# A fused LayerNorm, linear-attention and gated-MLP kernel: the first LayerNorm in eight groups of two tiles, without GpSimd's -mean*rs products, and a new order of the first tasks

## The chip, the cores and the metric

The kernel runs on one core of a Trainium2 chip. The time is the device time of one execution in microseconds, the median of the timed runs. A core has five engines that run their own queues of instructions in order and wait for each other by semaphores: PE (TensorE, matrix products; its weight loads are the profile's PEld), DVE (VectorE), ACT (ScalarE), POOL (GpSimd) and SP (SyncE, which here issues nearly all DMAs). Matrix products write to PSUM, eight banks; the rest lies in SBUF.

## The reference

x has 2048 rows (tokens) of 512; all inputs are bf16. With D = 512, 32 heads of 16 and F = 1376:

```python
mod = (_silu(c) @ w_mod).reshape(c.shape[0], 6, 1, -1)
sa, ca, ga, sb, cb, gb = (mod[:, i] for i in range(6))
h = _layernorm(x) * (1 + ca) + sa
x = x + ga * _A_ref(h, A_wqkv, A_w_phi, A_wo)
h = _layernorm(x) * (1 + cb) + sb
x = x + gb * _B_ref(h, B_w_gate, B_w_up, B_w_down)
```

_layernorm is (x - mean) / sqrt(var + 1e-5) over a row. _A_ref is linear attention: q, k and v are h @ wqkv; q and k go through w_phi, a 16x16 matrix for each head, and then phi = [softmax(p), softmax(-p)]; kv = phi_k^T v, z = the sum of phi_k, the output phi_q kv / (phi_q z), times wo. _B_ref is (sigmoid(h @ w_gate) * (h @ w_up)) @ w_down.

## The kernel before

The 2048 rows are 16 tiles of 128 rows. The work is a graph of some 1200 named tasks, each with an engine and a function that issues its instructions. Which engine runs a task, and in which order, is written out by hand in the string ORDER: Graph.arrange walks through it, takes for each task the engine behind "@" (A for ACT, D for DVE, P for POOL) or else the first one that the task allows, and gives each buffer a slot, the one that has been free longest in this order. So ORDER sets the queue of each engine, and also which task must wait for a PSUM bank until an earlier user of that bank is done. A task with no "@" runs on its first alternative: phi, wo, wd, and xn1 (but for tile 0) on POOL; qphi, n, r, hm1 and foldc as their tables say.

The stages at the start, with the names used below (t is a tile, g a group of tiles of the first LayerNorm, j a quarter of the 512 columns):

- ld_x0a to ld_x3a load x in pieces of 256 KB, two tiles each (ld_x3a is 512 KB, four tiles); ld_wk0 and ld_wk1 load the key weights, ld_wm00a to ld_wm01b the first columns of w_mod (256 KB each), ld_wv0 the value weights (512 KB). wqT0 to wqT3 load the query weights and transpose them in the DMA. All are issued by SP in ORDER's order.
- warm0 and warm1_i are matrix products without use on the zeroed last block of wd_sb, to keep PE busy.
- c1, c2, c3 make silu(c) on PE, ACT and DVE. modc1.0 and modc1.1 multiply it with w_mod on PE (16 products with one column each); modc1c0 and modc1c1 copy the results to modc.
- tpw transposes the key weights on PE, wTc copies them back, fold multiplies them with the block-diagonal w_phi, foldc copies the folded weights to wqk_f, so that K gives the features' logits directly. fold0 does the same for the query weights.
- st1_t (L702, L703, DVE) makes the mean and variance of tile t. rs1_g makes 1/sqrt(var + eps) for the tiles of a group: on ACT as Ln and Exp (L709, L710), on POOL as an addition and a power (L712, L713). nmr1_g (L718, DVE) makes -mean*rs, one instruction for each tile. xn1_t normalises a tile: on ACT or POOL as x*rs + nmr (L727, L731), on DVE, tile 0 alone, as (x - mean)*rs (L729).
- tphgj (L744) transposes column block j of a group on PE, all its tiles into one bank, and hm1_gj scales it with 1 + ca and adds sa on the way to h1T (L751 on ACT, L753 on DVE). Two groups (TD) are transposed by DMA (xT1_t) and scaled in place.
- K, V and Q are the products for tile t, four matmuls of 512 columns each; Kta and Ktb are the halves. e (ACT, L776) is exp of both signs from PSUM, n (DVE, L780) the sums over a head, r the reciprocal (DVE, or Ln and Exp on ACT), phi the product; va (ACT, L836) copies V out of PSUM. kv (PE, L282) adds phi^T v into two banks over all tiles.
- kvn and kvz (DVE) copy kv out; num, rd and u make the quotient for each tile, out multiplies with wo, and the MLP follows. Its loads are ld_wg0, ld_wu0, ld_wd; wo0 to wo3 (L851) scale wo by ga, on POOL.

The groups are

```python
LG = [[0], [1], [2, 3], [4, 5], [6, 7], [8, 9], [10, 11], [12, 13], [14, 15]]
TD = [0, 0, 0, 0, 0, 0, 1, 1, 0]
```

so tiles 0 and 1 are a group each, and from the third on a group's number is half its first tile plus one.

Of the kernel before, what the change touches and what calls it, by code (L numbers as in the profile page):

```python
# [160 lines left out]
def kernel(  # L161
# [535 lines left out]
    for g, ts in enumerate(LG):  # L697
# [17 lines left out]
        if g:  # L715
            def f_nm(e, ts=ts):
                for t in ts:
                    dve.tensor_scalar(nmr[:, 0, t:t + 1], mv1[:, t, 0:1], rs1[:, t:t + 1], -1.0, op0=ALU.mult, op1=ALU.mult)  # L718
# [340 lines left out]
```

## Time and profile before

| | |
|---|---|
| median of 3 timed runs | 203.72 us (203.69 to 203.81) |
| the profiled execution, its own time | 205.47 us |
| its span, first to last instruction | 203.7 us, 4159 instructions |
| mean granted TensorE clock | 0.992 |
| DMA | 22.94 MB, mean 113 GB/s |

One execution is recorded by the hardware profiler. Times in it count from the first instruction. "Busy" is the time in which an engine had an instruction under way; instructions overlap, so the sum of their durations is more. A timeline gives for each run of like instructions the start, the time, the line of the kernel, and in brackets the idle time before and what ended it. The chain of waits follows the end of the program back: each piece is what the next one waited for, or what stood before it on its engine. The profiled execution's own time is that of the whole execution, with what lies around its span.

### The profile page before, as it was taken

Reading aid. Unit: us, or ns where it says so; the run is one execution under the profiler, and the core shown is the slowest. Engines: PE = TensorE matmul, PEld = TensorE weight load, DVE = VectorE, ACT = ScalarE, POOL = GpSimd, SP = SyncE. Lnnn points to the kernel's source line nnn. Section 1 sums busy time; section 2 is a strip of 40 time slices with the busy share of each in tenths; the row PEclk is TensorE's granted clock in tenths of the full one; section 3 lists DMA queues with packets and bytes.
Section 4 is the critical chain, followed back from the end, with each engine's and each line's share of the span. In section 5 each row is a group of like instructions: output and inputs, shape, how many; then the busy total and the mean of one; then the engine's idle time right before and its main releaser. Section 6 shows DMA issues by size and latency. Waiting matters only on the chain.

```text
span 203.7 us, 4159 instructions
## 1 busy us (share of the span) xinstructions
PE 197.0 (97%) x1471; PEld 107.0 (53%) x1471; DVE 160.6 (79%) x375; ACT 106.1 (52%) x252; POOL 102.8 (50%) x144
## 2 busy tenths in 40 slices
...
PEclk9987999999999999999999999999999999999999
...
DMA packets 49453, 22.94 MB, mean 113 GB/s; under 512 B 38065, under 2 KB 47634, under 8 KB 49426
## 3 DMA queue, kind: packets, MB, share of 16 engines
...
q8 instruction: 13, 0.21, 0.5%
q14 instruction: 14, 0.11, 0.2%
q10 hardware_dynamic: 530, 0.02, 0.1%
HBM read 11.58 MB, written 2.10 MB: 67 GB/s over the span
## 4 chain that ended last, share of the span: by engine, by line
PE 79%; DMA 8%; ACT 5%; SPq 3%; DVE 3%; issue 1%
PE y_ps L485 19%; PE u_ps L447 18%; PE g_ps L447 17%; PE k_ps L817 6%; PE a_ps L356 6%; DMA wg_sb<-in_B_w_gate_dram 5%; PE v_ps L821 4%; DMA wmod_sb<-in_w_mod_dram 3%; PE q_ps L871 3%; ACT e L776 2%; PE num L326 2%; SPq L537 1%; PE g_ps L449 1%; PE tp_h L744 1%; PE kvacc L282 1%
## 5 line engine op out<-in xcount | busy, mean ns | idle before, releaser
L457 ACT ACTIVATE tg<-g_ps 128x512 bf16<-128x512 f32 (+5 forms) x66 | 28.8, 455 | 67.0 <-PE g_ps L447 39.4
L485 PE MATMUL y_ps<-wd_sb,wmod_sb 128*128 128x512 bf16 (+4 forms) x187 | 45.7, 366 | 0.0
L468 DVE SCALAR_TENSOR_TENSOR wmod_sb<-tg,u_ps 128x512 bf16<-128x512 bf16 (+4 forms) x63 | 30.2, 491 | 18.2 <-ACT tg L457 11.6
L447 PEld LDWEIGHTS <-wg_sb 128*128 128x128 bf16 (+1 forms) x252 | 21.9, 99 | 16.1
L447 PEld LDWEIGHTS <-wu_sb 128*128 128x128 bf16 (+1 forms) x252 | 21.9, 99 | 16.0 <-issue 0.3
L784 POOL TENSOR_TENSOR qphi<-qe,qks 128x512 bf16<-128x512 bf16 x24 | 25.1, 1060 | 3.9 <-DMA pT<-qphi 1.2
L485 PEld LDWEIGHTS <-wmod_sb 128*128 128x128 bf16 (+1 forms) x187 | 17.1, 98 | 16.0 <-issue 0.6
L447 PE MATMUL u_ps<-wT_sb,wu_sb 128*128 128x512 bf16 (+2 forms) x124 | 23.8, 322 | 0.0
L447 PE MATMUL g_ps<-wT_sb,wg_sb 128*128 128x512 bf16 (+2 forms) x124 | 23.1, 322 | 0.0
L447 PE MATMUL g_ps<-wqk_sb,wg_sb 128*128 128x128 bf16 (+4 forms) x128 | 20.0, 287 | 0.0
L447 PE MATMUL u_ps<-wqk_sb,wu_sb 128*128 128x128 bf16 (+4 forms) x128 | 19.8, 287 | 0.1
L780 DVE TENSOR_REDUCE ks<-e 128x64 f32<-128x1024 bf16 (+2 forms) x22 | 19.1, 904 | 0.4 <-ACT e L776 0.4
L780 DVE TENSOR_REDUCE qks<-qe 128x64 bf16<-128x1024 bf16 x16 | 19.2, 1204 | 0.0
L492 DVE TENSOR_TENSOR ot<-y_ps,x 128x512 bf16<-128x512 f32 (+2 forms) x17 | 11.0, 653 | 10.3 <-PE y_ps L485 10.2
L376 POOL TENSOR_SCALAR ve<-mv 128x2 f32<-128x2 f32 (+1 forms) x8 | 1.8, 221 | 33.8 <-DVE mv L366 33.7
L776 ACT ACTIVATE e<-k_ps 128x512 bf16<-128x512 f32 (+2 forms) x44 | 18.0, 515 | 0.0
L817 PE MATMUL k_ps<-wqk_f,h1T 128*128 128x512 bf16 x64 | 17.9, 402 | 0.0
L776 ACT ACTIVATE qe<-q_ps 128x512 bf16<-128x512 f32 x32 | 17.4, 618 | 0.6 <-POOL phi L787 0.4
L356 PE MATMUL a_ps<-wo_sb,oT 128*128 128x512 bf16 x64 | 16.3, 379 | 0.0
L787 POOL TENSOR_TENSOR phi<-e,kr 128x1024 bf16<-128x1024 bf16 (+2 forms) x10 | 14.4, 1449 | 3.6 <-ACT kr L795 2.1
L821 PE MATMUL v_ps<-wv_sb,h1T 128*128 128x512 bf16 x64 | 16.1, 379 | 0.0
L871 PE MATMUL q_ps<-wqk_f,h1T 128*128 128x512 bf16 x64 | 15.9, 379 | 0.0
...
## 6 DMA issues: line engine op xcount, KB each, us to landing
...
wu_sb<-in_B_w_up_dram SPq DMA_DIRECT2D x1, 1376.0 KB, 11.0
...
```

The lines of the kernel that those rows point to most:

```text
L356: pe.matmul(ap_[:], lhsT=oT[:, j, :], rhs=wo_sb[:, j, :], start=(j == 0), stop=(j == KT - 1))
L447: pe.matmul(ps[:fsz, 0:n], lhsT=w[:, j, ft * P:ft * P + fsz], rhs=h[:, j, 0:n], start=(j == 0), stop=(j == KT - 1))
L457: G.add(f"tg{k}.{ft}", {"ACT": 0.13 + n * 0.00083}, lambda e, tg=tg, g_ps=g_ps, fsz=fsz, n=n: act.activation(tg[:fsz, 0:n], g_ps[:fsz, 0:n ...
L468: dve.scalar_tensor_tensor(hm_all[:fsz, hm[k].slot, ft, 0:n], tg[:fsz, 0:n], 1.0, u_ps[:fsz, 0:n], op0=ALU.add, op1=ALU.mult)
L485: mm = pe.matmul(y[:, 0:c1 - c0], lhsT=hm_all[:fsz, hm[k].slot, ft, tl * P:(tl + 1) * P], rhs=wd_sb[:fsz, ft, c0:c1], start=(ft == 0), sto ...
L776: act.activation(ee[:, a:b, s].rearrange("p g f h -> p g (f h)"), kp[:, a * 64:b * 64].rearrange("p (g n) -> p g n", n=64), ACT.Exp, scale ...
L780: dve.tensor_reduce(ks[:, a:b].rearrange("p g s h -> p (g s) h"), ee[:, a:b].rearrange("p g s f h -> p (g s) h f"), axis=AX.X, op=ALU.add)
L784: engine(e).tensor_tensor(ph[:].rearrange("p (g s f h) -> p g s f h", s=2, f=DH, h=4)[:, :, s], ee[:, :, s], ks[:, :, 1 - s].unsqueeze(2). ...
L787: engine(e).tensor_tensor(ph[:, a * P:b * P].rearrange("p (g f h) -> p g f h", f=DH, h=4), ee[:, a:b].rearrange("p g s f h -> p (g s) f h" ...
L817: pe.matmul(kp[:], lhsT=h1T[:, j, t * P:(t + 1) * P], rhs=wqk_f[:, j, D:2 * D], start=(j == 0), stop=(j == KT - 1))
L821: pe.matmul(vp[:], lhsT=h1T[:, j, t * P:(t + 1) * P], rhs=wv_sb[:, j, :], start=(j == 0), stop=(j == KT - 1))
L871: pe.matmul(qp[:], lhsT=h1T[:, j, t * P:(t + 1) * P], rhs=wqk_f[:, j, 0:D], start=(j == 0), stop=(j == KT - 1))
```

## The change

Tiles 0 and 1 become one group, so there are eight groups of two, and a group's number is half its first tile; tiles 10 to 13 still go through the DMA transposes. rs1_0 now waits for both tiles' statistics. A single product nmr1, for tile 1, is left: tile 1 is normalised by ACT, tile 0 by DVE, and all others by POOL, which now computes (x - mean)*rs from the statistics and no longer x*rs + nmr. warm1 has 13 tasks, not 12. The tasks ahead of wd0, 439 before and 424 after, stand in a new order, with some engines changed; behind them the order is the same.

```diff
-LG = [[0], [1], [2, 3], [4, 5], [6, 7], [8, 9], [10, 11], [12, 13], [14, 15]]
-TD = [0, 0, 0, 0, 0, 0, 1, 1, 0]
+LG = [[t, t + 1] for t in range(0, NT, 2)]
+TD = [0, 0, 0, 0, 0, 1, 1, 0]
...
 ORDER = """
-wdz pmem warm0 ld_x0a st1_1 rs1_1 st1_0 c1 c2 ld_x0b warm1_0 warm1_1 warm1_2 warm1_3 ld_wk0 ld_wk1 nmr1_1 xn1_1@A st1_3 warm1_4 st1_2 rs1_0 xn1_0 tph11 tpw1
-tpw0 ld_x1b ld_x1a wTc1 warm1_5 tpw2 ld_wm00b c3 tph10 tph03 tph00 st1_7 tpw3 bd rs1_2@P tph13 wTc0 nmr1_2 xn1_3 xn1_2 warm1_6 ld_wm00a st1_6 wTc2 st1_4 st1_5
-wTc3 fold11 fold10 warm1_7 foldc11 ld_x2b fold13 warm1_8 st1_11 foldc10 fold12 warm1_9 foldc13 modc1.0 warm1_10 ld_wm01b tph20 foldc12 warm1_11 rs1_4@P nmr1_4
-ld_wm01a modc1c0 hm1_11@A hm1_10@A tph02 rs1_3@P tph01 tph23 hm1_20@A hm1_01@A st1_10 tph21 hm1_21@A hm1_00 modc1.1 modc1c1@D rs1_6 nmr1_3 tph22 tph12 ld_x2a
-wqT1 hm1_22 hm1_13@A hm1_03 xn1_7 K1a K0a hm1_02@A hm1_23@A xn1_6 tph42 tph40 xn1_5 hm1_40@A st1_8 tph41 ld_x3a xn1_4 K3a hm1_42 hm1_12@A ld_wv0 nmr1_6 tph43
-K3b hm1_41@A xn1_11 tph30 xn1_10 st1_9 rs1_5@P hm1_30@A tph31 wqT3 tph32 K1b ld_wmga st1_15 st1_14 hm1_31@A fold01 foldc01 K0b tph33 wqT2 rs1_8@P K2a K2b hm1_33
-nmr1_5 V0a wqT0 V0b V3a xn1_9 e3.0 V1a xT1_11 e0.0 fold03 n3.0 V1b nmr1_8 xn1_14 va0 e2.0 n0.0 st1_13 r0.0 modca.0 modca.1 xn1_15 st1_12 xn1_8 foldc03 n2.0
-modcac e1.0 hm1_32@A V2a fold02 phi0.0 n1.0 r1.0 fold00 V2b foldc02 foldc00 r3.0 va1 xT1_10 hm1_60@P ld_wmm2 va2 r2.0@A hm1_62@P tph82 hm1_82@A tph50 phi2.0@D
-phi1.0@D hm1_50@A hm1_63@P V3b K4a K4b rs1_7@P Q0 Q2 kv0.0 Q1 qe0.0 va3 qe2.0 hm1_43@A qe1.0 modc2.0 tph52 modc2.1 tph51 nmr1_7 xn1_12 xn1_13 phi3.0@D ld_wo
-qn0.0 modc2c e4.0 kv1.0 qn2.0 hm1_52 kv2.0 Q4 K5a kv3.0 xT1_12 xT1_13 qphi0.0@P qphi0.1@P qn1.0 qe4.0 qphi2.1 tph80 K5b hm1_80@A hm1_51@A e5.0 pT0 qphi2.0 n4.0
-r4.0@A qn4.0 n5.0 phi4.0@D qphi1.1@P hm1_61@P qphi1.0@P tph53 V5 K7a V4 va5 hm1_53@A V6 pT2 hm1_70@P qphi4.1 va4 hm1_71 mask4 va6 K6a K7b K6b e6.0 K8 tph83
-hm1_83 r5.0 qphi4.0@P e8.0 pT1 pT4 ld_wd2 tph81 hm1_81 n6.0 n8.0 e7.0 n7.0 V7 kv4.0 hm1_72@P K11 K9 V9 K14 V8 r6.0@A e9.0 va7 va9 r7.0@A e11.2 e11.6 phi5.0
-phi6.0 hm1_73@P n9.0 r9.0@A kv5.0 gwa gra gwb e11.4 e14.0 K10 phi7.0@D kv6.0 K12 V10 kv7.0 e14.4 r8.0 n11.6 n11.2 r11.6 phi9.0 e10.0 e12.0 ld_wd ld_wu0 grb
-n11.4 n14.0 r11.2 n14.4 r14.0 n10.0 r14.4@A phi8.0 va8 V11 V14 n12.0 e11.0 K13 n11.0 phi11.6 r11.4 wo1 r11.0 va10 r10.0@A va11 kv8.0 kv9.0 phi11.2@D phi11.0@D
-phi10.0@D phi11.4@D V12 K15 e13.0 wmod_free ld_wg0 phi14.4 phi14.0 kv10.0 kv11.4 kv11.6 Q6 kv11.0 e13.4 r12.0@A e15.4 n13.0 n13.4 r13.0 r13.4 n15.4 e15.0 va14
-V15 V13 qe6.0 va12 kv11.2 n15.0 r15.0 r15.4@A va13 phi13.4 Q5 phi15.4 phi13.0@D va15 phi15.0@D phi12.0@D wo0 wo3 Q3 kv12.0 kv13.0 kv14.0 kv15.0 qn6.0 kvn0 kvz0
-kv13.4 kv14.4 kv15.4 kvz1 kvn1 num0a num1a num2a wo2 rd0a wo_all rd1a qe3.0 u0a num0b num4a num1b rd0b Q11 qe5.0 rd2a u0b u2a rd4a num2b qn3.0 u1a rd1b tpo0 Q8
-qphi6.0@P qphi6.1@P oT0 out0 num4b rd2b u1b wd0 qe11.0 u2b qphi3.1@P qphi3.0@P x1_0 rd4b st2_0 qe8.0 Q7 qe7.0 tpo1 oT1 Q10 Q9 out1 Q15 oT2 rs2_0 qn5.0 nmr2_0
...
+wdz pmem bd warm0 ld_x0a ld_x0b c1 st1_0 st1_1 rs1_0 warm1_0 st1_3 nmr1 xn1_1 c2 st1_2 rs1_1@P xn1_3 xn1_2 warm1_1 warm1_2 warm1_3 warm1_4 warm1_5 ld_wk0 tpw0
+wTc0 tpw1 wTc1 warm1_6 ld_x1a warm1_7 warm1_8 warm1_9 ld_wk1 tpw3 c3 warm1_10 wTc3 xn1_0 tph00 tpw2 fold11 wTc2 fold10 fold13 foldc10 foldc13 ld_x1b fold12
+tph01 warm1_11 st1_5 foldc12 st1_4 rs1_2@P xn1_4 xn1_5 st1_7 foldc11 st1_6 rs1_3 xn1_7 xn1_6 warm1_12 tph13 ld_x2b tph10 tph11 ld_wm00b ld_wm00a modc1.0 st1_11
+modc1c0@D hm1_11 tph22 hm1_10 ld_wm01b hm1_01@A tph20 tph12 hm1_20@A st1_10 rs1_5@P xn1_11 xn1_10 ld_wm01a hm1_00@A tph03 tph02 modc1.1 modc1c1@D hm1_13 K3a
+hm1_02@A hm1_03@A ld_x3a st1_15 ld_x2a st1_8 K0a st1_14 rs1_7@P hm1_12@A hm1_22@A tph23 K1a K2a K0b e0.0 ld_wv0 K3b st1_9 rs1_4@P xn1_8 K1b e1.0 e3.0 V3a V3b
+tph21 tph30 V0a st1_13 V0b va0 hm1_21 hm1_23 n0.0 K2b e2.0 tph32 hm1_32 K5a wqT2 fold02 foldc02 va3 hm1_30@A V1a V2a r0.0 V1b wqT3 wqT0 fold03 foldc03 wqT1
+fold01 foldc01 fold00 tph31 V2b n2.0 foldc00 va2 n3.0 xT1_11 st1_12 xn1_9 tph43 xn1_15 xn1_14 va1 xT1_10 r2.0@A K4a K4b tph72 hm1_72 n1.0 r1.0 phi0.0 hm1_50@P
+hm1_52@P hm1_51@P hm1_31@A rs1_6@P xn1_13 xn1_12 Q0 qe0.0 Q2 hm1_43@A qe2.0 kv0.0 phi2.0@D K5b ld_wmga Q1 phi1.0@D modca.0 modca.1 qn0.0 qe1.0 kv1.0 r3.0
+phi3.0@D modcac e5.0 V4 qn1.0 kv2.0 e4.0 ld_wmm2 modc2.0 tph33 hm1_33@A kv3.0 qphi0.1@P xT1_13 tph40 qn2.0 qphi2.0 qphi0.0@P hm1_40@A tph41 hm1_41@A gwa modc2.1
+modc2c xT1_12 va4 Q4 qe4.0 pT0 qphi2.1@P n4.0 tph42 V6 r4.0@A hm1_42 n5.0 K6a K6b qn4.0 hm1_53 phi4.0@D va6 qphi1.1@P qphi1.0@P pT2 ld_wd2 hm1_61@P qphi4.1
+tph70 K8 hm1_70@A r5.0 mask4 qphi4.0@P tph71 e6.0 n6.0 V5 va5 V9 pT1 e8.0 hm1_71 n8.0 pT4 kv4.0 K7a K7b e7.0 K9 V7 V11 e9.0 r6.0@A va9 va7 K11 e11.4 n7.0 r7.0@A
+n9.0 hm1_63@P hm1_62@P phi5.0 tph73 hm1_73 kv5.0 K10 phi6.0 V8 phi7.0@D hm1_60@P kv6.0 K14 V10 kv7.0 e11.0 r9.0@A phi9.0 e11.2 n11.4 n11.0 n11.2 r11.2 e10.0
+r8.0 r11.4@A e14.0 e11.6 n10.0 n11.6 n14.0 r14.0 va8 e14.4 K12 e12.0 phi8.0 r11.0 K15 r11.6 K13 n14.4 va11 n12.0 kv8.0 kv9.0 phi11.4@D Q6 V12 r10.0@A phi11.0@D
+phi11.2@D e13.4 r14.4@A phi10.0@D e13.0 va10 n13.0 n13.4 V14 r13.4 r13.0 ld_wo gwb gra wo1 va12 e15.4 e15.0 phi11.6 phi14.4 kv10.0 kv11.4 qe6.0 phi14.0 r12.0@A
+n15.4 r15.4@A kv11.0 kv11.2 Q5 V15 kv11.6 V13 n15.0 r15.0 phi13.0@D phi12.0@D va14 phi15.0@D phi13.4 Q3 va13 qn6.0 kv12.0 va15 kv13.0 kv14.0 kv15.0 phi15.4
+kv13.4 kv14.4 kv15.4 kvz0 kvn0 num0a kvz1 kvn1 num1a rd0a u0a qe5.0 num0b rd0b u0b num4a num2a Q8 rd4a wo2 num2b tpo0 num1b qe3.0 Q11 wo3 rd1a u1a wo0 oT0
+ld_wg0 wo_all grb ld_wd out0 num4b rd2a u2a wmod_free rd1b qn3.0 rd2b ld_wu0 qphi6.0@P u1b qphi6.1@P wd0 qe11.0 u2b qphi3.1@P qphi3.0@P x1_0 rd4b st2_0 qe8.0 Q7
...
                 pe.matmul(ps[:], lhsT=wd_sb[:, FT - 1, 0:P], rhs=wd_sb[:, FT - 1, :], start=True, stop=True)
         G.add(nm, {"PE": dur}, f, bufs=[ps], **kw)
     warm("warm0", 6, 2.4, r=["wdz"], w=["warm"])
-    for i in range(12):
+    for i in range(13):
         warm(f"warm1_{i}", 1, 0.22, r=["c1"], w=["warm"])
 
     def modc_task(nm, chs, rks, wk, f2, dur):
...
                 pool.tensor_scalar(ve1[:, sl], mv1[:, sl, 1], 1e-5, None, op0=ALU.add)
                 pool.tensor_tensor(rs1[:, sl], ve1[:, sl], mhalf[:, sl], op=ALU.pow)
         G.add(f"rs1_{g}", {"ACT": 0.43, "POOL": 1.1}, f_rs, r=[("mv1", t) for t in ts], w=[("rs1", g)])
-        if g:
-            def f_nm(e, ts=ts):
-                for t in ts:
-                    dve.tensor_scalar(nmr[:, 0, t:t + 1], mv1[:, t, 0:1], rs1[:, t:t + 1], -1.0, op0=ALU.mult, op1=ALU.mult)
-            G.add(f"nmr1_{g}", {"DVE": 0.02 + 0.1 * n}, f_nm,
+        if g == 0:
+            G.add("nmr1", {"DVE": 0.12}, lambda e: dve.tensor_scalar(nmr[:, 0, 1:2], mv1[:, 1, 0:1], rs1[:, 1:2], -1.0, op0=ALU.mult, op1=ALU.mult),
                   r=[("rs1", g)], w=[("nmr1", g)])
         for t in ts:
             xn = Buf("xn", [P, D], BF16, "xn")
...
             def f_xn(e, t=t, xn=xn):
                 if e == "ACT":
                     act.activation(xn[:], x_sb[:, t, :], ACT.Identity, scale=rs1[:, t:t + 1], bias=nmr[:, 0, t:t + 1])
-                elif e == "DVE":
-                    dve.tensor_scalar(xn[:], x_sb[:, t, :], mv1[:, t, 0:1], rs1[:, t:t + 1], op0=ALU.subtract, op1=ALU.mult)
                 else:
-                    pool.tensor_scalar(xn[:], x_sb[:, t, :], rs1[:, t:t + 1], nmr[:, 0, t:t + 1], op0=ALU.mult, op1=ALU.add)
-            G.add(f"xn1_{t}", {"POOL": 0.69, "ACT": 0.73} if t else {"DVE": 0.3}, f_xn, r=[("rs1", g)] + ([("nmr1", g)] if t else []), w=[("xn1", t)],
+                    engine(e).tensor_scalar(xn[:], x_sb[:, t, :], mv1[:, t, 0:1], rs1[:, t:t + 1], op0=ALU.subtract, op1=ALU.mult)
+            G.add(f"xn1_{t}", {"ACT": 0.73} if t == 1 else {"POOL": 0.69} if t else {"DVE": 0.3}, f_xn, r=[("rs1", g)] + ([("nmr1", g)] if t == 1 else []), w=[("xn1", t)],
                   bufs=[xn], port=("POOL", "DVE"))
         if TD[g]:
             for q, t in enumerate(ts):
```

58 lines of the change are left out of this document (29 added, 29 removed).

## The prediction

> **What bounds the kernel now.** First the page's busy shares and its row of the granted TensorE clock, in 40 slices of 5.1 us.
>
> ```profile
> span 203.7 us, 4159 instructions
> PE 197.0 (97%) x1471; PEld 107.0 (53%) x1471; DVE 160.6 (79%) x375; ACT 106.1 (52%) x252; POOL 102.8 (50%) x144
> PEclk9987999999999999999999999999999999999999
> ```
>
> PE is busy 97% of the span, and its clock dips only in slices 2 and 3. The windows, cut at that dip, show the stages (columns: length, busy of PE, PEld, DVE, ACT, POOL, clock, DMA share, GB/s).
>
> ```profile
> 10.85:14.26 3.41, 2.92 (x48) 1.85 (x47) 3.23 (x14) 3.12 (x11) 3.24 (x7) 1.00 1.26 218
> 14.26:17.68 3.42, 3.42 (x16) 1.76 (x15) 3.14 (x10) 2.54 (x7) 2.60 (x5) 0.50 1.15 345
> 17.68:24.20 6.52, 6.52 (x63) 3.92 (x61) 5.33 (x14) 6.07 (x14) 5.20 (x9) 1.00 1.25 217
> 24.20:25.10 0.90, 0.71 (x5) 0.27 (x4) 0.86 (x3) 0.90 (x3) 0.68 (x2) 1.00 1.06 403
> 25.10:58.60 33.50, 33.50 (x315) 18.37 (x315) 33.29 (x60) 32.62 (x92) 27.70 (x28) 1.00 0.73 201
> 77.00:190.00 113.00, 113.00 (x714) 59.63 (x712) 84.13 (x193) 37.58 (x77) 39.05 (x56) 1.00 0.32 62
> ```
>
> From 17.68 on PE never rests, but for the stretch at 24.2. From 25.1 to 58.6 three engines are full at once: PE 33.50 of 33.50, DVE 33.29, ACT 32.62. So time can come only from the first 25 us, and whatever PE gains there lasts only if DVE and ACT gain as much. The chain of waits says what starts the work.
>
> ```profile
> 7.07 6.14 DMA wmod_sb<-in_w_mod_dram
> 13.26 0.55 PE modc_ps L630 x16
> 13.81 0.33 PE tp_h L744 x3
> 14.14 1.46 PE k_ps L817 x4
> 15.60 0.64 PE tp_h L744 x6
> ...
> 25.08 0.27 PE tp_h L744 x2
> ...
> 25.78 0.86 PE k_ps L817 x4
> ```
>
> The eleventh load of 256 KB (ld_wm01a) lands at 7.07 + 6.14 = 13.21; modc1.1 needs it, and K1a follows at 14.14. Four K matmuls take 0.86 at 25.78: 0.215 each, or 0.43 at half clock. A transpose takes 0.64 / 6 = 0.107 at half clock, so 0.054 at full. The half-clock stretch, 3.42 us of a full PE, costs 1.7 us.
>
> **The change part by part.** Prices (groups by shape up to 58.6 us: busy, mean ns, idle before), then pitches from the timelines, where one instruction starts before the last has ended.
>
> ```profile
> L718 DVE TENSOR_SCALAR nmr<-mv,rs 128x1 f32<-128x1 f32 x15 | 2.4, 200 | 0.0
> L753 DVE TENSOR_SCALAR h1T<-tp_h,modc 128x256 bf16<-128x256 bf16 x6 | 2.3, 389 | 0.9 <-PE tp_h L744 0.9
> L753 DVE TENSOR_SCALAR h1T<-tp_h,modc 128x128 bf16<-128x128 bf16 x2 | 0.7, 334 | 0.0
> L731 POOL TENSOR_SCALAR xn<-x_sb,rs,nmr 128x512 bf16<-128x512 bf16 x14 | 11.0, 796 | 3.6 <-DVE nmr L718 1.4 <-issue 1.2 <-ACT h1T L751 0.8
> L729 DVE TENSOR_SCALAR xn<-x_sb,mv,rs 128x512 bf16<-128x512 bf16 x1 | 0.4, 382 | 0.0
> L787 POOL TENSOR_TENSOR phi<-e,kr 128x512 bf16<-128x512 bf16 x4 | 4.2, 1075 | 2.3 <-ACT kr L795 1.3 <-DVE phi L787 1.0
> ```
>
> ```profile
> 5.33 0.18 DVE L718 TENSOR_SCALAR nmr<-mv,rs 128x1 f32<-128x1 f32 x1
> 5.42 0.68 DVE L702 BATCH_NORM_STATS2 st<-x_sb 128x6 f32<-128x512 bf16 x1
> ...
> 6.24 0.66 DVE L702 BATCH_NORM_STATS2 st<-x_sb 128x6 f32<-128x512 bf16 x1
> ```
>
> ```profile
> 5.54 0.81 ACT L727 ACTIVATE xn<-x_sb,nmr,rs 128x512 bf16<-128x512 bf16 x1 [0.24 <-DVE nmr L718]
> 7.11 2.05 ACT L664 COPY wT_sb<-tp_w 128x512 bf16<-128x512 bf16 x4 [0.34 <-PE tp_w L661]
> 9.11 2.20 ACT L685 CAST wqk_f<-fold_ps 128x512 bf16<-128x512 f32 x4
> 13.74 0.31 ACT L709 ACTIVATE ve<-mv,eps 128x2 f32<-128x2 f32 x1
> 14.08 0.20 ACT L710 ACTIVATE rs<-ve 128x2 f32<-128x2 f32 x1
> 14.19 1.24 ACT L751 ACTIVATE h1T<-tp_h,modc 128x128 bf16<-128x128 bf16 x3
> 19.51 2.08 ACT L776 ACTIVATE e<-k_ps 128x512 bf16<-128x512 f32 x4
> ```
>
> *DVE.* Fourteen of 15 nmr go. One holds DVE between 0.09 (5.33 to 5.42) and 0.16 us (2.4 / 15); I take 0.11, which is 0.09 under the mean of 200 ns: -1.55. The scalings h1T on DVE go from 6 pairs of tiles and 2 single tiles to 10 pairs; with the same 0.09 off their means +4 x 0.30 - 2 x 0.25 = +0.7. modc1c0 comes over from ACT, one small instruction (+0.1, as nmr), and one of tile 11's reciprocals goes to ACT (-0.15, an estimate from nmr's 0.11). Sum: -0.9.
>
> *ACT.* Six single-tile scalings go, 14 pairs stay; three take 1.24 with the last one's overlap, some 0.38 each: -2.3. One pair of Ln and Exp goes (13.74 to 14.19): -0.45; modc1c0's two small instructions -0.25, between that pair's pitches of 0.34 and 0.11; the reciprocal is a Ln and an Exp, +0.45. Sum: -2.5. Earlier on, ACT loses: rs1_0 now waits for both tiles' statistics and xn1_1 for an nmr1 that stands behind st1_3, a statistic of 0.82 (5.42 to 6.24). So xn1_1 starts near 6.45, not 5.54; behind it wait c2, wTc0 and three more copies, then foldc10. What the 0.34 idle before 7.11 doesn't absorb, and ld_wk1 landing one place later, makes foldc10 start near 9.55, not 9.11, and the fourth foldc end near 11.5. That is hidden as long as modc1.0 waits for its load anyway: its two loads go one place back behind ld_x2b, one place is about 0.8 us (13.21 is the eleventh), so the ninth lands near 11.5.
>
> *POOL.* Without nmr, POOL's 1.4 of waits on it go, and xn1_3 follows rs1_1. subtract-then-multiply doesn't occur on POOL here. Bounds: 382 ns (DVE, the same form) and 1075 ns (POOL, two tensors); I take 0.77, the nearest row (L731, the same tile and engine). Then xn1_3 and xn1_2 end near 9.7, rs1_2 near 10.9 (DVE's st1_4 at 9.85), xn1_5 near 12.4.
>
> *SP and DMA.* Ahead of ld_wm01a stand the same ten loads of 256 KB, so it lands at 13.2 again. ld_wv0 passes one transposing load: behind 13.21 come 512 + 256 + 512 KB, at 345 GB/s 3.8 us, so 17.0; V3a, its first user, comes at 18.6. ld_wo waits on SP behind the transposes pT4, and ld_wg0, ld_wd, ld_wu0 go close behind it. I price them at nothing:
>
> ```profile
> 50.62 1.16 POOL L851 TENSOR_TENSOR wo_sb<-wo_sb,ga_sb 128x512 bf16<-128x512 bf16 x1
> 69.49 0.61 PE L447 MATMUL g_ps<-wqk_sb,wg_sb 128*128 128x128 bf16 x8
> ```
>
> wo is first used at 50.6, wg and wu at 69.5, and SP is past pT4 near 40. Without that cover 512 KB would cost 1.5 us.
>
> *PE.* One warm matmul more, in idle time: 0. K3a stands right behind modc1.1: 13.81 against 14.14, **-0.33**. By then 20 transposes are behind PE (00 to 03, 10 to 13, 20, 22, two each), against 16 now: 4 x 0.054 = **-0.21**. The stall at 24.2 (the transposes of 25.08 come late) is a bank: tph50 reuses the one that hm1_32 frees on ACT. In the new order fold00, tph31 and K4a stand there and reuse those of foldc02, va3 and foldc03, which ACT passes 0.4 to 0.8 us before. Of the 0.90 us the five matmuls (two V, partly earlier, and three transposes) are worth 2 x 0.215 + 3 x 0.054 = 0.59 at most and 0.38 with one V, so 0.31 to 0.52 is lost; I take **-0.4**. Sum -0.94.
>
> Can DVE and ACT follow? ACT has 2.5 less. Its first e starts when K0b ends: with the half-clock stretch where it is, K3a, K0a, tph23, K1a, K2a, K0b end near 17.75, against 19.51 now. DVE has only 0.9 less, yet it idles 1.19 from 17.68 to 24.20 (5.33 of 6.52) and 0.28 in the window before; by its queue phi2 and phi1 end near 28.5, about 1 us earlier than now. Walking the queues on, the tight places are Q0 (25.4, its bank from foldc00 at 25.1), Q4 (32.4, e4.0 at 32.5), V6 (33.5, hm1_33 at 33.0), K8 (35.3, hm1_42 at 34.7), kv4.0 (38.05, phi4.0 at 37.8). None costs more than 0.1. From wd0 on both orders agree, and PE is full (113.00 of 113.00 from 77 to 190): the lead goes through to the end.
>
> **Against the time.** The profiled execution took 205.47, its span is 203.7, so 1.8 lies around it; the median of the timed runs is 203.72, 1.75 less than that execution. I take the difference off the median: 203.72 - 0.94 = **202.8**.
>
> **A rule of the Trainium skill.** Rows first:
>
> ```profile
> 11.36 0.38 PE L600 MATMUL warm<-wd_sb 128*128 128x512 bf16 x1
> 11.90 0.38 PE L600 MATMUL warm<-wd_sb 128*128 128x512 bf16 x1
> ```
>
> The clock is 0.50 for 3.42 us from 14.26, behind a stretch in which PE counts as 2.92 of 3.41 busy, mostly with transposes and one-column matmuls. The Trainium skill, "TensorE: Matmul & The Clock Gate", says that the gate judges free-running windows of 3413 ns (Part 1, "What's actually happening") and that transposes don't count as PE-busy in the same way (Part 4, "PE-mode transpose"). The trace agrees in the length; no run here shows the phase of other executions. By that rule the new order, whose warm matmuls stand ahead of tph13 and end near 10.1, keeps the half-clock stretch or gets a worse one; the time would be 202.8 in the first case and that of the third rival in the second.
>
> **Rivals.**
> 1. *The half-clock stretch goes or is shorter.* PE gains up to 1.7 more, but DVE gains only 0.8 (its statistics of tiles 8 to 15 wait for loads and end near 18.9): 203.7 - 0.95 - 0.8 to 1.7 = 201.5. Against it: from 10.85 to 14.26 the new order has two warm matmuls fewer (those at 11.36 and 11.90), against 0.4 us more of K. Chance 0.10.
> 2. *The tight banks slip.* The five margins are 0.1 to 0.5 us. If DVE or ACT is late by 0.3 at two of them, PE loses most of the lead, 203.4; if POOL's new form costs 1.0 rather than 0.77, xn1_5 is 0.9 late, tph22 holds PE's queue, and modc1.1 and K3a behind it lose some 0.65: 203.5. For it: full DVE and ACT. Chance 0.28 (0.07 of it still faster by over 0.2%, 0.17 the same, 0.04 slower).
> 3. *Slower: two half-clock stretches in a row.* If PE's work from 14.26 to 17.68 isn't enough to lift the clock, 17.68 to 21.1 runs at half too, with K and V on PE: +1.7 - 0.95, so 204.5. It decides where K0a to K0b wait for ACT's hm1_00 to hm1_03 (near 13.7 to 15.2): if those are over a microsecond late, PE idles in the window. Against it: now this window, full of K, lifts the clock. Chance 0.10.
> 4. *It does nothing*, because every gain of PE is given back to a full DVE: 203.7. Against it: DVE's own sum is -0.9. Chance 0.04.
>
> **How the numbers follow.** Forecast 202.8, from 202.2 to 203.2, chance 0.48. A measurement of this kernel can tell 0.2% (0.4 us) from no change. Faster by more: 0.48 + 0.10 + 0.07 = 0.65 and so 0.67 with the edge of the fourth; same 0.17 + 0.02 = 0.19; slower 0.10 + 0.04 = 0.14. The range for 8 in 10 is 201.7 to 203.8: it takes in the nearer half of the first rival and all of the second that isn't slower.
>
> **What would show it.**
>
> ```profile
> 57.62 1.19 PE L282 MATMUL kvacc<-vaug,phi 128*128 128x68 bf16 x32
> ```
>
> Right: K3a starts at 13.8 behind modc1.1; the first e at about 17.8; no PE gap at 24.2; the last 32 kvacc matmuls start near 56.7, not where this row has them; the half clock at the same place. Wrong: tph22 waiting for POOL's xn after 12.5, L731's mean above 0.85, a clock of 0.50 past 17.7, or PE gaps behind hm1_42, phi4.0 or foldc00 of over 0.3 us.

## The result: 221.36 us, slower by 8.5%, and the profile after

| | before | after |
|---|---|---|
| time, median (4 runs each, same chip) | 203.76 us (203.69 to 205.83) | 221.36 us (221.32 to 221.75) |
| ratio after / before, 95% interval | | 1.0852 [1.0811, 1.0894] |
| span of the profiled execution | 203.7 us | 219.5 us |

The forecast was 202.8 (201.7 to 203.8), so it was wrong in sign and in size. First the page of the changed kernel: span, busy shares, and in 40 slices of 5.5 us the row of PE's busy tenths and that of its granted clock.

```profile
span 219.5 us, 4110 instructions
...
PE 200.7 (91%) x1447; PEld 108.7 (50%) x1472; DVE 160.6 (73%) x362; ACT 104.4 (48%) x244; POOL 122.6 (56%) x145
...
PE   7827945999999999999999999999999999999992
...
PEclk9965995599999999999999999999999999999999
```

POOL is the one engine with much more to do: 122.6 us against 102.8. Counted from 0, PE rests most in slices 2, 5 and 6, and the clock falls twice, over two slices each time; before, it fell once and by less. From slice 7 on PE is full as before. The groups of the same page (busy us, mean ns, idle before and its releaser) name what POOL does:

```profile
L725 POOL TENSOR_SCALAR xn<-x_sb,mv,rs 128x512 bf16<-128x512 bf16 x14 | 29.0, 2079 | 0.5
...
L738 PE MATMUL tp_h<-ident,xn 128*128 128x128 bf16 x48 | 6.8, 256 | 11.2 <-POOL xn L725 11.2
```

POOL's normalising of a tile takes 2079 ns in place of 796, 14 times: 14 x 1.283 = 18.0 of POOL's 19.8 more. PE's transposes wait 11.2 us for it. POOL's timeline from 8 us on (start, length, instructions) shows that nothing else holds it:

```profile
8.25 4.14 POOL L725 TENSOR_SCALAR xn<-x_sb,mv,rs 128x512 bf16<-128x512 bf16 x2
12.36 0.23 POOL L711 TENSOR_SCALAR ve<-mv 128x2 f32<-128x2 f32 x1
12.68 0.72 POOL L712 TENSOR_TENSOR rs<-ve,mhalf 128x2 f32<-128x2 f32 x1
13.50 8.25 POOL L725 TENSOR_SCALAR xn<-x_sb,mv,rs 128x512 bf16<-128x512 bf16 x4
```

xn1_3 starts at 8.25, where the prediction's walk along the queues had it (near 8.2). Two of the new instructions end at 12.39 and not at 9.7, the next four, back to back, at 21.75. PE's timeline over the same time and further, with the idle time before an instruction and its releaser in brackets:

```profile
12.45 0.77 PE L738 MATMUL tp_h<-ident,xn 128*128 128x128 bf16 x6 [2.17 <-POOL xn L725]
...
15.63 0.29 PE L738 MATMUL tp_h<-ident,xn 128*128 128x128 bf16 x1 [2.01 <-POOL xn L725]
17.69 1.14 PE L738 MATMUL tp_h<-ident,xn 128*128 128x128 bf16 x9 [1.77 <-POOL xn L725]
...
31.20 0.23 PE L738 MATMUL tp_h<-ident,xn 128*128 128x128 bf16 x1 [1.35 <-POOL xn L725]
33.26 0.29 PE L738 MATMUL tp_h<-ident,xn 128*128 128x128 bf16 x1 [1.83 <-POOL xn L725]
...
37.37 0.39 PE L738 MATMUL tp_h<-ident,xn 128*128 128x128 bf16 x2 [2.11 <-POOL xn L725]
```

Each wait ends when one POOL instruction ends, and the six add up to the 11.2 us. tph22's two transposes stand at 15.63 and 17.69, and behind them in PE's queue stand modc1.1 and K3a, which was forecast at 13.8 and comes at 19.1. Around these waits the clock falls; the windows (length, busy of PE, PEld, DVE, ACT, POOL, clock, DMA share, GB/s) of the two stretches:

```profile
12.60:22.90 10.30, 6.30 (x58) 3.98 (x58) 5.12 (x15) 3.51 (x7) 9.93 (x8) 0.51 0.63 137
33.10:43.30 10.20, 7.93 (x28) 3.15 (x29) 4.26 (x6) 2.62 (x5) 10.01 (x10) 0.50 0.23 90
```

POOL is full, DVE and ACT starve at half load or less, and PE's 14.23 us of work runs at half clock. The same work at full clock would take 7.1 us less; with the 11.2 us of waits that makes 18.3 against the 17.6 us lost, an upper estimate, since some of the slow work hides behind POOL anyway. The Trainium skill, "TensorE: Matmul & The Clock Gate" (Part 1, "What's actually happening"), judges windows of 3413 ns; some 10.2 us of half clock are three of them, which agrees. Its table of states there puts the half clock behind an idle window of that length; here no wait for POOL is longer than 2.2 us, and yet the clock falls, so the waits need not fill a window.

Last, the first product of the attention's quotient, which needs all of kv, on PE's timeline:

```profile
73.73 0.97 PE L325 MATMUL num<-kvb,pT 128*128 128x68 bf16 x20 [0.33 <-DVE kvb L293]
```

From there to the end of the span are 145.8 us. In the profile of the kernel before without its half-clock stretch, shown below (num at 57.45, span 202.0), they are 144.6, so nearly all is lost ahead of the first num. Of the 1.2 us behind it, 1.0 is the last store, which lands in 2.5 us in place of 1.5; the section on the quick form comes back to that.

### The profile page after: what moved, and what is told of

It reads as the page before. It is cut to its first block, busy times and chain, and to the rows that moved or that the text cites. A ratio compares the mean times of both kernels' runs of the same rounds, so it can differ in the third digit from the quotient of the medians.

```text
span 219.5 us, 4110 instructions
## 1 busy us (share of the span) xinstructions
PE 200.7 (91%) x1447; PEld 108.7 (50%) x1472; DVE 160.6 (73%) x362; ACT 104.4 (48%) x244; POOL 122.6 (56%) x145
## 4 chain that ended last, share of the span: by engine, by line
PE 67%; DVE 12%; POOL 9%; ACT 6%; issue 3%; DMA 1%; POOLq 0%; ACTq 0%; DVEq 0%
PE y_ps L484 17%; PE u_ps L446 16%; PE g_ps L446 16%; POOL xn L725 7%; PE a_ps L355 5%; ACT e L770 4%; DVE ks L774 4%; PE q_ps L865 3%; PE k_ps L811 2%; PE num L325 2%; DVE phi L781 2%; DVE qks L774 2%; DVE st L701 1%; DMA x_sb<-in_A_x_dram 1%; PE g_ps L448 1%
## 5 line engine op out<-in xcount | busy, mean ns | idle before, releaser
L484 PE MATMUL y_ps<-wd_sb,wmod_sb 128*128 128x512 bf16 (+4 forms) x180 | 44.2, 366 | 0.2
L467 DVE SCALAR_TENSOR_TENSOR wmod_sb<-tg,u_ps 128x512 bf16<-128x512 bf16 (+4 forms) x63 | 30.2, 491 | 18.4 <-ACT tg L456 11.5
L725 POOL TENSOR_SCALAR xn<-x_sb,mv,rs 128x512 bf16<-128x512 bf16 x14 | 29.0, 2079 | 0.5
L778 POOL TENSOR_TENSOR qphi<-qe,qks 128x512 bf16<-128x512 bf16 x25 | 26.3, 1068 | 3.4 <-DMA pT<-qphi 1.4
L446 PE MATMUL u_ps<-wqk_sb,wu_sb 128*128 128x128 bf16 (+4 forms) x127 | 19.8, 286 | 0.2 <-ACT qe L770 0.2
L811 PE MATMUL k_ps<-wqk_f,h1T 128*128 128x512 bf16 x62 | 18.6, 432 | 0.3 <-issue 0.2
L865 PE MATMUL q_ps<-wqk_f,h1T 128*128 128x512 bf16 x59 | 17.9, 423 | 0.2
L738 PE MATMUL tp_h<-ident,xn 128*128 128x128 bf16 x48 | 6.8, 256 | 11.2 <-POOL xn L725 11.2
```

Of the source, the lines that this page charges most:

```text
L446: pe.matmul(ps[:fsz, 0:n], lhsT=w[:, j, ft * P:ft * P + fsz], rhs=h[:, j, 0:n], start=(j == 0), stop=(j == KT - 1))
L467: dve.scalar_tensor_tensor(hm_all[:fsz, hm[k].slot, ft, 0:n], tg[:fsz, 0:n], 1.0, u_ps[:fsz, 0:n], op0=ALU.add, op1=ALU.mult)
L484: mm = pe.matmul(y[:, 0:c1 - c0], lhsT=hm_all[:fsz, hm[k].slot, ft, tl * P:(tl + 1) * P], rhs=wd_sb[:fsz, ft, c0:c1], start=(ft == 0), sto ...
L725: engine(e).tensor_scalar(xn[:], x_sb[:, t, :], mv1[:, t, 0:1], rs1[:, t:t + 1], op0=ALU.subtract, op1=ALU.mult)
L778: engine(e).tensor_tensor(ph[:].rearrange("p (g s f h) -> p g s f h", s=2, f=DH, h=4)[:, :, s], ee[:, :, s], ks[:, :, 1 - s].unsqueeze(2). ...
L811: pe.matmul(kp[:], lhsT=h1T[:, j, t * P:(t + 1) * P], rhs=wqk_f[:, j, D:2 * D], start=(j == 0), stop=(j == KT - 1))
```

## The experiments

A pair (a, b) below names the two operations of one tensor_scalar: a with its first column operand, then b with the second. The kernel before has (mult, add) on POOL, the changed one (subtract, mult). Theory: POOL's new pair of operations is dear, and that alone makes the kernel slower. Rivals: the new order itself (groups, places in the queues), or what the instruction reads (mean and rs as columns of two tiles, the mean with a stride) in place of the operations. In all experiments the kernel before ran beside: medians 203.88, 203.91 and 203.92 in the three sets.

### The old order with the new form, and the new order without it

*Old order, new form.* The kernel before, with one line changed:

```diff
-pool.tensor_scalar(xn[:], x_sb[:, t, :], rs1[:, t:t + 1], nmr[:, 0, t:t + 1], op0=ALU.mult, op1=ALU.add)
+pool.tensor_scalar(xn[:], x_sb[:, t, :], mv1[:, t, 0:1], rs1[:, t:t + 1], op0=ALU.subtract, op1=ALU.mult)
```

> The kernel before, in its old order with all nmr products and waits kept, but POOL computes (x - mean)*rs. A: POOL xn 2.07 us each, 14 x 1.3 = 18.2 us more on POOL, time 215 to 222. B: xn may be slow but the old order hides most of it, under 208.

Measured: 219.75 us (219.68 to 220.35), ratio 1.0776 [1.0726, 1.0827]. The waits of PE up to 90 us, longest in total first (total, times, longest):

```profile
PE tp_h L744 <- POOL xn L731: 8.6, 6, 1.8
```

This is case A: POOL's mean is 2079 ns here too. The one line costs 15.9 us in the old order, with the old groups and with the products still made.

*New order, same operands, other operations.* The changed kernel, where POOL computes x*mean + rs, so that tiles 2 to 15 are not normalised:

```diff
-engine(e).tensor_scalar(xn[:], ..., mv1[:, t, 0:1], rs1[:, t:t + 1], op0=ALU.subtract, op1=ALU.mult)
+ops = (ALU.mult, ALU.add) if e == "POOL" else (ALU.subtract, ALU.mult)
+engine(e).tensor_scalar(xn[:], ..., mv1[:, t, 0:1], rs1[:, t:t + 1], op0=ops[0], op1=ops[1])
```

> The changed kernel as it is, with only the two operations on POOL exchanged: x*mean + rs in place of (x - mean)*rs, the same operands and waits. Tiles 2 to 15 are thus not normalised. A1 (the pair of operations is what is dear): xn 0.77 us, time 202.3 to 203.5. A2 (the operand is what is dear: the mean lies 8 bytes apart in mv, nmr 4): xn stays at 2.07, time 221.

Measured: 204.54 us (204.27 to 206.16, 10 runs), ratio 1.0033 [1.0009, 1.0058]. POOL's group, then its windows cut as above:

```profile
L726 POOL TENSOR_SCALAR xn<-x_sb,mv,rs 128x512 bf16<-128x512 bf16 x14 | 10.6, 773 | 0.5
```

```profile
12.60:22.90 10.30, 10.27 (x89) 5.99 (x90) 10.06 (x23) 9.97 (x22) 9.62 (x15) 1.00 1.17 238
33.10:43.30 10.20, 10.17 (x68) 4.95 (x67) 10.16 (x16) 9.95 (x30) 9.20 (x10) 1.00 0.84 155
```

With the same tiles read in the same way, 773 ns; PE, DVE and ACT are full where they starved, and the clock is 1.00. So the operations make the price, not the operands, as A1 has it, and in the new order they cost 221.36 - 204.54 = 16.8 us. The time missed A1's 202.3 to 203.5: what is left of the change, +0.66 us in this set, is no gain. It is taken up below.

### Which pairs are dear

The kernel before, with seven pairs on POOL, two tiles each, all on the same operands rs and nmr:

```diff
+elif t in (3, 8):
+    pool.tensor_scalar(xn[:], x_sb[:, t, :], rs1[:, t:t + 1], nmr[:, 0, t:t + 1], op0=ALU.subtract, op1=ALU.mult)
...
```

> The kernel before with seven pairs of operations on POOL, two tiles each, the same operands rs and nmr: (mult, add), (subtract, mult), (add, mult), (mult, subtract), (mult, mult), (subtract, subtract), (add, add). Tiles 2 to 15 are thus not normalised but for tiles 2 and 9. If subtract as such is dear, the three pairs with subtract take about 2.07 and the others 0.77; if one pair alone is quick, (mult, add) takes 0.77 and all others 2.07; if a multiplication in second place is dear, (subtract, mult), (add, mult) and (mult, mult) do.

The groups of POOL up to 90 us, in the order of their busy time: L741 is (subtract, subtract), L733 (subtract, mult), L737 (mult, subtract), L743 (add, add), L739 (mult, mult), L731 (mult, add) and L735 (add, mult).

```profile
L741 POOL TENSOR_SCALAR xn<-x_sb,rs,nmr 128x512 bf16<-128x512 bf16 x2 | 4.7, 2341 | 0.4 <-DVE nmr L718 0.4
...
L733 POOL TENSOR_SCALAR xn<-x_sb,rs,nmr 128x512 bf16<-128x512 bf16 x2 | 4.2, 2086 | 0.8 <-POOL rs L713 0.8
L737 POOL TENSOR_SCALAR xn<-x_sb,rs,nmr 128x512 bf16<-128x512 bf16 x2 | 4.2, 2080 | 0.0
L743 POOL TENSOR_SCALAR xn<-x_sb,rs,nmr 128x512 bf16<-128x512 bf16 x2 | 4.2, 2090 | 0.0
L739 POOL TENSOR_SCALAR xn<-x_sb,rs,nmr 128x512 bf16<-128x512 bf16 x2 | 1.5, 768 | 0.0
L731 POOL TENSOR_SCALAR xn<-x_sb,rs,nmr 128x512 bf16<-128x512 bf16 x2 | 1.5, 768 | 0.0
L735 POOL TENSOR_SCALAR xn<-x_sb,rs,nmr 128x512 bf16<-128x512 bf16 x2 | 1.5, 767 | 0.0
```

There are two classes: 767 or 768 ns, and 2080 ns or more. Every tried pair with a subtract is dear, in either place, and so is (add, add); three pairs of add and mult are quick. None of the three rules expected fits all seven, and why (add, add) is dear stays open. The Trainium skill, "GPSIMD Engine Reference", section 3.1, gives 1.8 cycles an element at 1.2 GHz, 768 ns for 512 elements, as the best case of a tight unrolled loop without branches that depend on the data. The quick pairs agree with it; the dear ones take 2.080 x 1.2 / 512 x 1000 = 4.9 cycles, an estimate by the same clock, for which that section has no row. One execution of this kernel, with eight dear tiles, took 214.14 us.

### Is it the half clock?

The changed kernel, with 34 more matmuls without use in PE's queue, ahead of the four transposes that wait for POOL, so that PE idles less:

```diff
+for i, n in enumerate((8, 9, 7, 10)):
+    warm(f"warm2_{i}", n, 0.22 * n, r=["c1"], w=["warm"])
```

> The changed kernel (xn at 2.07 us) with 34 more matmuls without use, put on PE in its four longest waits for POOL (ahead of tph13, tph22, tph43 and tph72), to hold the clock. If POOL's queue alone sets the time, the clock rises but the time stays within 0.5 us of 221.4. If the half-clock stretches cost of their own where PE works behind POOL's last xn of tiles 14 and 15 (about 14 matmuls at 0.21 us more), 218 to 219.5.

One execution took 225.11 us, 3.7 more than the changed kernel, with a mean clock of 0.987 where it had 0.953. Both expectations missed. The waits are filled in part: PE still waits 6.5 us for POOL, up to 2.0 at a time, in place of 11.2. With that the half clock shrinks from two stretches to one of 3.4 us (a clock of 0.83 from 30 to 40 us), so it does go with PE's idling. But the first num comes at 74.0, no earlier than 73.73, and 3.5 us are lost behind it, where PE now waits 1.4 us for POOL (L423) and 1.1 for the DMA transpose of o; in the changed kernel no wait there is longer than 0.2. What the half clock costs by itself isn't settled, since the added matmuls also take PE's time and turns in the banks: in the waits of PE up to 90 us there is now also

```profile
PE k_ps L813 <- DVE h1T L749: 1.7, 1, 1.7
```

### Why the new order doesn't gain even with a quick form

*The kernel before, once more, unchanged.*

> The kernel before, unchanged, for a profile at full clock: most of its timed runs show a granted clock of 1.0 and a span of 201.9 to 202.4, the profiled one of the prediction 0.992 and 203.7. If the half-clock stretch is worth 1.7, the first num comes near 57.4 here (59.2 there) and PE's last matmul near 198.8 (200.5). If the kernel with x*mean + rs in the new order is ahead by the predicted 0.9 in its first 57 us, its first num (56.97) stands 0.9 before this one's; if its lead is smaller, the terms of PE's sum were too large.

One execution took 203.76 us, with a span of 202.0 us. Its page has no half-clock stretch, and the num and the last matmul stand where they were expected:

```profile
PEclk9999999999999999999999999999999999999999
```

So it is the partner for the run with the same operands. The first K and the first num on PE's timeline, of the kernel before and then of the new order with (mult, add):

```profile
13.75 1.02 PE L817 MATMUL k_ps<-wqk_f,h1T 128*128 128x512 bf16 x4
...
57.45 0.93 PE L326 MATMUL num<-kvb,pT 128*128 128x68 bf16 x24 [0.36 <-DVE kvb L299]
```

```profile
13.63 1.07 PE L812 MATMUL k_ps<-wqk_f,h1T 128*128 128x512 bf16 x4
...
56.97 0.97 PE L325 MATMUL num<-kvb,pT 128*128 128x68 bf16 x20 [0.33 <-DVE kvb L293]
```

PE's lead is 0.48 us at the first num. The last matmul starts at 198.58 against 198.79, so 0.20 of it is left; yet the span is 1.0 longer, 203.0 against 202.0. The rest lies in the last store. DMAs of the window from the last store's issue on, first before (199.5 to 203), then the new order with (mult, add) (199.3 to 203.1): queues with packets, MB and share, and issues with KB and us to landing.

```profile
q1 hardware_dynamic: 294, 0.17, 15.9%
issues: line engine op xcount, KB each, median us to landing
out_dram<-ot SPq DMA_DIRECT2D x1, 32.0 KB, 1.5
```

```profile
q1 hardware_dynamic: 293, 0.17, 14.5%
q14 instruction: 1, 0.01, 1.0%
issues: line engine op xcount, KB each, median us to landing
out_dram<-ot SPq DMA_DIRECT2D x1, 32.0 KB, 2.7
```

A fetch of instructions, 8 KB, falls beside the last store, and the store lands 1.2 us later. The new order's DVE issues 13 instructions fewer (362 against 375), so a fetch at a fixed place of DVE's program would come later in time. Three runs try that, the third with -mean on DVE further below.

*Thirteen DVE instructions given back*, at 169 to 171 us of the span, on the new order with (mult, add):

```diff
+for t in ts[:1 if g == 6 else 2]:
+    dve.tensor_scalar(fil[:, t:t + 1], mv1[:, t, 0:1], -1.0, None, op0=ALU.mult)
```

> The run with the same operands and (mult, add) on POOL (204.54 us; tiles 2 to 15 not normalised) with 13 small DVE instructions whose result nobody reads, some 25 us ahead of the end, so that DVE again issues 375. Nothing ahead of them changes. If an instruction fetch of the shorter DVE program makes the last store late: no instruction packet beside the last store, 32 KB landing in 1.5 to 1.6 us instead of 2.7, and 203.2 to 203.6 us. If the late piece has another cause: 2.7 us still and 204.4 to 204.8.

The DMAs from 201.2 to 204 us; the last store is issued at 201.3:

```profile
q1 hardware_dynamic: 296, 0.17, 20.5%
issues: line engine op xcount, KB each, median us to landing
out_dram<-ot SPq DMA_DIRECT2D x1, 128.0 KB, 1.7
out_dram<-ot SPq DMA_DIRECT2D x1, 32.0 KB, 1.5
```

The fetch comes at 200.19, ahead of that store, and it lands in 1.5 us, as expected. The times fall into two groups, six of 203.26 to 203.91 (median 203.62) and six of 205.09 to 205.59; the whole is 204.5, ratio 1.0019 [0.9991, 1.0048]. The first group lies about the forecast of 203.2 to 203.6; the time alone isn't proof, since half of the executions lie above it, but the landing of the store bears it out. The profiled one is of the second: there the value weights land at 18.4, not 16.1, and PE waits (waits of PE, 8 to 60 us):

```profile
PE v_ps L822 <- DMA wv_sb<-in_A_wqkv_dram: 1.4, 1, 1.4
```

Five of the second group have a mean clock of 0.992. Why so many executions of this kernel are disturbed at the start stays open.

*The products taken away in the old order.* POOL computes x*mean + rs, and DVE makes no nmr1_2 to nmr1_8:

```diff
-        if g:
+        if g == 1:
             def f_nm(e, ts=ts):
```

> The kernel before, in its own order and groups, with POOL computing x*mean + rs (tiles 2 to 15 not normalised) and without the 14 products on DVE: the opposite of the run with the fillers. If the shorter DVE program moves a fetch onto the last store: an instruction packet beside it, 2.7 us to landing, and 204.6 to 205.2 us, although the products' work is gone. If not: 203.4 to 204.0. Beside the run of the old order with -mean on POOL (205.67) it also says what those 7 small POOL instructions cost: about 0.9 us if the first num returns to 57.4 to 57.6 from 58.4.

204.56 us (204.44 to 205.25, 11 runs), ratio 1.0031 [1.0008, 1.0055]: less work, and slower. The first num, then the DMAs behind the issue of the last stores (199.5 to 203):

```profile
57.47 0.92 PE L326 MATMUL num<-kvb,pT 128*128 128x68 bf16 x24 [0.36 <-DVE kvb L299]
```

```profile
q14 instruction: 1, 0.01, 0.7%
issues: line engine op xcount, KB each, median us to landing
...
out_dram<-ot SPq DMA_DIRECT2D x1, 32.0 KB, 2.3
```

PE is where it was (57.47 against 57.45), and the store lands 0.8 us late beside a fetch. Removing the 14 products gained PE nothing and cost 0.6 us at the end: the products had been hidden behind other work. With the fillers' run the late store is shown from both sides: 14 DVE instructions fewer bring it, 13 more take it away. All fourteen profiles of this case agree: in the six whose DVE issues 361 or 362 instructions, an 8 KB fetch stands behind the last store's issue and the store lands in 2.3 to 2.8 us; in the eight with 375 or 376 there is none, and it lands in 1.5 or 1.6. That the fetch is DVE's own is not shown, since the trace doesn't name its engine, and in the new order 13 instructions move it by little: from 1.1 us behind the store's issue (200.48 and 199.37) to 1.1 us ahead of it (200.19 and 201.30).

### Are there forms that give the same numbers and beat the kernel before?

*Product and quick form back, in the new order* (seven nmr1 of two tiles each, put just ahead of their xn1; xn1_3, xn1_2 and others moved behind them in the order):

```diff
-rs1_1@P xn1_3 xn1_2 warm1_1 ... wTc3 xn1_0 tph00
+rs1_1@P warm1_1 ... wTc3 xn1_0 nmr1_1 xn1_3 xn1_2 tph00
...
```

> The changed kernel (groups of two, new order), but POOL normalises as x*rs + nmr again, with seven nmr1 products back on DVE, placed where DVE passes them soon after rs1. Theory A (POOL's subtract-then-multiply costs 2.07 us where multiply-then-add cost 0.77, and all of the 17.6 us come from it): xn on POOL back at 0.77, time 202.6 to 203.8. Rival B (the new order and its bank waits lose time by themselves): over 206, with PE waiting at other places than xn.

206.28 us (206.2 to 206.37), ratio 1.0106 [1.0061, 1.0151]. POOL's xn is back at 788 ns, but theory A's time missed, and the time is rival B's, over 206: with the quick form the new order is 2.4 us behind the kernel before. All four runs have a mean clock of 0.992. The window of that stretch:

```profile
14.60:17.90 3.30, 3.30 (x26) 1.54 (x25) 3.11 (x11) 2.33 (x5) 2.29 (x5) 0.53 1.95 177
```

PE is full there, at 0.53: the half-clock stretch that the kernel before has in some executions, this one has in all four. It is worth some 1.7 us of the 2.4: the first num comes at 59.76, and at 59.17 in the kernel before with that stretch. Why it stands in each execution here stays open.

*The pair (add, mult), (x + (-mean)) times rs, with -mean from seven small POOL instructions*, in the new order and in the old:

```diff
+pool.tensor_scalar(nm1[:, sl], mv1[:, sl, 0], -1.0, None, op0=ALU.mult)
+pool.tensor_scalar(xn[:], x_sb[:, t, :], nm1[:, t:t + 1], rs1[:, t:t + 1], op0=ALU.add, op1=ALU.mult)
```

> The changed kernel, with POOL computing (x + (-mean))*rs, the pair (add, mult), in place of (x - mean)*rs; -mean for a group's two tiles is one more small instruction on POOL, seven in all at some 0.25 us. Theory A (the pair of operations alone): xn 0.77 us, time 204.3 to 205.0, as with x*mean + rs (204.54); more if POOL's seven small ones come on the path, up to 205.5. Rival (something else in the group's tasks): xn above 1 us, time over 210.

> The kernel before in its old groups and old order, with (x + (-mean))*rs on POOL and without the 14 products on DVE: this part of the change alone, in a form that costs 0.77. If DVE's 1.55 us count, 203.0 to 203.5 against 203.88; if PE sets the pace, 203.6 to 204.0.

New order 207.02 us (206.63 to 208.25), ratio 1.0154 [1.0119, 1.0188]; old order 205.67 (205.56 to 205.88), ratio 1.0081 [1.0055, 1.0108]. Both missed, on the slow side, though xn takes 767 ns in both, so that here too the pair alone makes its price. In the new order the profile has a half-clock stretch again, from 14.0 to 17.4 us, and the last store lands in 2.5 us. In the old order the small instructions and the first num are

```profile
L735 POOL TENSOR_SCALAR nm<-mv 128x2 f32<-128x2 f32 x7 | 1.6, 224 | 0.3
```

```profile
58.44 0.93 PE L328 MATMUL num<-kvb,pT 128*128 128x68 bf16 x24 [0.36 <-DVE kvb L301]
```

The run without products that has no such instructions has its num at 57.47. So 1.6 us of small work on POOL, ahead of its xn, go with a PE that is 0.97 late; the last store adds its 0.9 (2.4 us to landing).

*-mean on DVE*, in the places of the products (old order), and behind the statistics (new order):

```diff
-dve.tensor_scalar(nmr[:, 0, t:t + 1], mv1[:, t, 0:1], rs1[:, t:t + 1], -1.0, op0=ALU.mult, op1=ALU.mult)
+dve.tensor_scalar(nmr[:, 0, t:t + 1], mv1[:, t, 0:1], -1.0, None, op0=ALU.mult)
```

> The kernel before, in its own order and groups; in the places of the 14 small products on DVE stand 14 small negations (-mean, one input), and POOL computes (x + (-mean))*rs, a pair that took 767 ns. The number of DVE instructions stays, POOL issues nothing more, and POOL's normalising no longer waits for a DVE result that itself waits for POOL's rs. Theory A (the way over DVE cost little, PE is bound by its own work): 203.6 to 204.0, no difference that can be measured. Theory B (that way over DVE held PE's early transposes): 202.8 to 203.5. Theory C (the pair (add, mult) with two inputs that are columns of different tiles hides a cost, as the run of the old order with -mean on POOL, 205.7, could be read): about 205 or more.

> The changed kernel with POOL's pair (x + (-mean))*rs and 14 small negations on DVE right behind the statistics of each group: everything is computed, and DVE issues one instruction more than in the kernel before. If the last store's late piece belongs to the shorter DVE program (its instruction fetch falls on that store), it lands in 1.5 to 1.6 us and the time is 203.2 to 203.8; if it belongs to the new order, 2.7 us and 204.4 to 205.0.

Old order 203.9 us (203.62 to 205.43), ratio 0.9988 [0.9958, 1.0018]: no difference. This is theory A: the kernel no longer sends -mean*rs from POOL's rs over DVE back to POOL, so that way cost next to nothing. New order 205.24 (204.74 to 205.94), ratio 1.0069 [1.0049, 1.0089]: the store lands in 1.5 us, as the theory of the fetch has it, but the time missed its 203.2 to 203.8. Six of its eleven executions have the half-clock stretch (a mean clock of 0.992); the other five took 204.74 to 205.11. From the new order, a row of DVE's groups and one of PE's timeline:

```profile
L720 DVE TENSOR_SCALAR nmr<-mv 128x1 f32<-128x1 f32 x14 | 1.6, 147 | 0.2
```

```profile
58.16 0.97 PE L325 MATMUL num<-kvb,pT 128*128 128x68 bf16 x20 [0.33 <-DVE kvb L293]
```

Against 56.97 the num is 1.2 us late, with 1.6 us more on DVE ahead of it. PE waits 0.8 us for DVE's phi here and not at all for it with (mult, add), while its waits for POOL are 0.9 us in both: so in the new order DVE is tight at the start, and 14 small instructions are paid almost in full. No version that computes everything is measurably faster than the kernel before.

## Why the prediction was wrong, point by point

- **The step that failed** is POOL's: "subtract-then-multiply doesn't occur on POOL here. Bounds: 382 ns (DVE, the same form) and 1075 ns (POOL, two tensors); I take 0.77, the nearest row (L731, the same tile and engine)." It measured 2.08, nearly twice the upper bound of 1.075. L731 (796 ns in its row, 0.77 by the prediction's reading) was the nearest by tile, type and engine, but not by operations, and on POOL these decide (768 ns or 2080 in one kernel, on the same operands). This one term is 15.9 us in the old order and 16.8 in the new. A pair of operations for which the trace has no row had no upper bound in it, and the range should have said so.
- **The mechanism behind the price was seen.** The second rival had POOL late, tph22 holding PE's queue, and modc1.1 and K3a behind it; the wrong signs named were tph22 waiting after 12.5, a mean above 0.85 and a half clock past 17.7. All three came. It was priced with 1.0 us for the instruction, and so at 203.5.
- **Third rival, half-clock stretches in a row:** they came, but with PE's waits for POOL, not for ACT's hm1, and each about three times as long as the 3.42 us before.
- **PE's lead of 0.94** is judged by the run with (mult, add), at full clock: 0.48 at the first num. K3a starts at 13.63 there, near the forecast of 13.8; but the kernel before, without its half-clock stretch, has K1a at 13.75 on the same timeline (13.98 in the profile of the prediction, whose 14.14 is a row of the chain), so -0.33 shrinks to -0.12. K does stand 0.44 closer behind modc1.1, but modc1.1 starts at 13.22 and not at 12.90: even with the quick form tph22's two transposes, ahead of it in PE's queue, wait 0.9 us for POOL, the last until 12.63. That is the second rival's path, at the price of 0.77. The stall at 24.2 doesn't go so much as move: PE's gaps of over 60 ns (from one matmul's start to the next, less what its columns take) from 14 us to the last kvacc add up to some 0.8 before and 0.7 in the new order, -0.1 in place of -0.4. This is rough, as some matmul records are missing from both traces. With the -0.21 for four more transposes, which nothing here measures alone, the sum is about -0.4.
- **"The lead goes through to the end"** failed: 0.28 of it is lost in PE behind the first num, and the last store costs up to 1.2. The prediction expected nothing behind wd0, because both orders agree there; it didn't weigh that fewer DVE instructions can go with a fetch beside the last store.
- **DVE's -1.55 for the products** bought nothing in the old order (57.47 against 57.45). In the new one, 14 instructions like them cost 1.2: the new order needs the products gone and still gains nothing on the kernel before by it.
- **The time against the median** was right: before without its half-clock stretch has span 202.0, so the profile of before was 1.7 long.
